# Chunk 1's d_ff tiles 4 to 7 by seven products for eight, chunk 0's block tiles moved ahead of them, and one block's token sums on VectorE

## The chip, the cores and the metric

The kernel runs on one core of one Trainium2 chip. The metric is the device time of one execution in microseconds; the time of the kernel before is the median of three runs. Beside these runs one execution was taken with the hardware profiler, and its trace carries all the rows below.

## The reference

Two stages follow each other. The first is an attention with sketched features, for 4 batches, 4 heads, 1088 tokens and 32 numbers a head; the second is a feed-forward layer with an exact GELU on the 4352 tokens of width 128 that the first one gives.

```python
phi(x) = outer(S1 @ x, S2 @ x)                # 8 x 8 = 64 features a token and head
kv = sum over s of phi(k[s]) v[s];  z = sum over s of phi(k[s])
x  = (phi(q) @ kv) / (phi(q) @ z + 1e-6)      # [4, 4, 1088, 32] -> x [4352, 128]
h  = x @ w_in                                 # [4352, 2048]
out = (0.5 * h * (1 + erf(h / sqrt(2)))) @ w_out   # [4352, 128]
```

`w_in` and `w_out` come as 64-bit floats (the setup multiplies by a 64-bit scalar), so the kernel turns them into 32-bit floats itself, out of their words.

## The kernel before

**Chunks, tiles, steps.** Tokens are worked on in nine chunks: two of 512 tokens for each of the 4 batches (chunks 0 to 7), and one of the 256 tokens left over. For each chunk d_ff is cut into 16 tiles of 128 channels. One *step* t of the main loop is one tile of one chunk: `hidden` (L734; its matmul is L740) multiplies a w_in tile with the chunk's 512 tokens into one of two PSUM banks (`hps`, two buffers), and ScalarE's GELU (L747) takes the bank to SBUF. The list `steps` gives the order of the tiles. Before, it is: chunk 0's tiles 0 to 3 (t = 0 to 3), chunk 1's tiles 0 to 7 (t = 4 to 11), chunk 0's tiles 4 to 15 (t = 12 to 23), chunk 1's tiles 8 to 15 (t = 24 to 31), then the 16 tiles of chunk 2, and so on.

**Two ways for the second product.** The first `USUAL[n]` tiles of chunks 0 and 1 (4 and 8 of them before) go through `project` (L914; matmul L925): one 128x512 product a tile, summed in one bank. All other tiles of chunks 0 to 7 go in *blocks* of four tiles (`NB = 4`) by a scheme with seven products for eight. It needs, for each block, four sums of the tokens' activations (`token_sums`, L783, four GpSimd subtractions or additions of 128x512, L791 to L794) and, for each piece of w_out, four sums of the channels' weights (`channel_sums`, L768, into the tiles `T[1]` to `T[4]`, L778 to L781; the last one, `T[4]`, is needed by the first product of a block). `two_products` (L813, matmul L826) issues two of the 14 products of a block beside each other on the two halves of the array. The two accumulating banks come from the same two-buffer pool (`ops`) as the banks of `project`, so `take_usual` (L852) first copies the usual products away on ScalarE. `drain` (L831) and `combine` (L856) undo the scheme.

**Where the steps' work is put.** Each engine gets its instructions in the order of the text, and keeps that order. `at(t, f, ...)` hangs a call into the list of step t; calls hung into the same step are issued in the order in which the `at` lines stand. In one step the order is: drains, `hidden` with its GELU, `token_sums` of a block whose last tile this was, the step's list, stores, and last the products of `project` and `two_products` that were put into this step.

**The weights.** w_in and w_out lie in five pieces of d_ff (tiles 0-1, 2-3, 4-7, 8-11, 12-15). Pieces 0 and 1 are converted ahead of the loop and in its first steps, pieces 2, 3 and 4 by the list `schedule` (L1146). A piece takes two VectorE instructions on its words (`begin`: L283, L288), two on ScalarE (L270 `low`, L294 `exp`), and three more on VectorE (`end`: L302, L307, L312). The last step of the last piece, the product that makes w_out's tiles 12 to 15, is GpSimd's (`multiply`, L312, hung into step 13). The raw words of pieces 2 to 4 lie in the three buffers of `block`, which the activations of the blocks take over, in that order.

**Around them.** In the same stretch the keys and queries of batch 1 are worked on: `key_turn_blocks` (L383), `features_of_all` (L1043), `outer_of_all` (L1051 to L1058), `turn_keys_rem` and `features_rem` (L348, L421), `add_tokens` (L1067 to L1073), `query_turn` (L554), `z_sum`, `fold_z`, `kv_and_attend` (L456), `query_sketch` (L604), `query_outer` (L616 to L639). `hidden` issues its matmul in two halves of 64 columns from t = 18 on.

The lines that settle GpSimd's order in the stretch of the change:

```python
    at(12, widen_v_rem, 1)
    at(13, multiply, turns[5])
    for i, t in enumerate((5, 6, 14)):
        at(t, channel_sums, i)
    at(16, channel_sums, 3)
```

Of the kernel before, what the change touches and what calls it, by code (L numbers as in the profile page):

```python
# [16 lines left out]
def kernel(  # L17
# [18 lines left out]
    pe, dve, act, pool, sp = nc.tensor, nc.vector, nc.scalar, nc.gpsimd, nc.sync  # L36
# [15 lines left out]
    LAG = 2  # L52
    NMAIN = B * NCH
    NB = 4

    USUAL = [4, 8]
    BLOCKED = 12
    NCHUNK = NMAIN + 1
    assert B == 4 and d_model == 128 == H * D == JC * D == 2 * F and H == 4 and REM == 64 and NCH == 2
# [8 lines left out]
    def work_banks():  # L68

        return wps.tile([128, 2, CW], FP, name="w_ps")  # L70
# [99 lines left out]
    def words(a):  # L170

        return (a, 1) if a.dtype == FP else (a.bitcast(U32), 2)
# [22 lines left out]
    for i, (queue, s) in enumerate(((act, S1), (sp, S2))):  # L195
        s, e = words(s)
# [286 lines left out]
    def turn_kv(b, banks):  # L483

        for rows in (slice(0, 64), slice(64, 128)):
            pe.matmul(banks[rows, 1, :128], lhsT=kv_T[b], rhs=ident, start=True, stop=True)
        act.copy(out=kz[b], in_=banks[:, 1, :128])
# [246 lines left out]
    def hidden(n, fi, by_halves=False):  # L734
# [3 lines left out]
        for rows in (slice(0, 64), slice(64, 128)) if by_halves else (slice(0, 128),):  # L738
            if (n, fi) not in begun:
                pe.matmul(ps[rows, :W], lhsT=w[:, rows], rhs=xT[n][:, :W], start=True, stop=True)  # L740
        if n < NCH and fi < USUAL[n]:
            g_of[n, fi] = mlp.tile([128, CW], FP, name="g", bufs=4)
# [37 lines left out]
        pool.tensor_sub(out=t2, in0=b22, in1=t1)  # L780
        pool.tensor_sub(out=t4, in0=b21, in1=t2)  # L781

    def token_sums(n, b):  # L783

        g = blocks[n, b].rearrange("p (e two) (half x) -> p e two half x", two=2, half=2)
        a11, a21, a12, a22 = (g[:, :, k, h] for k in range(2) for h in range(2))
        s = {}
        for j, (name, dtype) in enumerate((("bits_a", U32), ("bits_e", U32), ("bits_low", FP), ("bits_m", FP))):
            t = mlp.tile([128, LC], dtype, name=name, bufs=3 if dtype == U32 else 2)
            s[j + 1] = (t if dtype == FP else t.bitcast(FP)).rearrange("p (e x) -> p e x", e=2)  # L790
        pool.tensor_sub(out=s[3], in0=a11, in1=a21)  # L791
        pool.tensor_add(out=s[1], in0=a21, in1=a22)  # L792
        pool.tensor_sub(out=s[2], in0=s[1], in1=a11)  # L793
        pool.tensor_sub(out=s[4], in0=a12, in1=s[2])  # L794
        sums[n, b] = s

    def factor(n, b, name, e):
# [12 lines left out]
    def first_block(n):  # L810
        return USUAL[n] // NB if n < NCH else 0

# [39 lines left out]
    def take_usual(n):  # L852
        usual[n] = mlp.tile([128, CW], FP, name="g", bufs=4)
        act.copy(out=usual[n], in_=o_of[n])
# [59 lines left out]
    def project(n, fi, parts=range(B // 2), cols=slice(None)):  # L914
        first, final = fi == (BLOCKED if n == NMAIN else 0), fi == (USUAL[n] if n < NCH else NF) - 1
        if first and n not in o_of:
# [78 lines left out]
    late = []  # L995
# [32 lines left out]

    steps = [(n, fi) for n in range(NCH) for fi in range(USUAL[n])]
    steps += [(n, fi) for n in range(NCHUNK) for fi in range(USUAL[n] if n < NCH else 0, NF)]  # L1030
    slots = {t: [] for t in range(len(steps) + LAG)}

    def at(t, f, *a):
        slots[t].append(lambda: f(*a))
# [40 lines left out]
    held = {}  # L1075
# [67 lines left out]

    turns = [w[i] for i in range(2, 5) for w in (w_in_sb, w_out_sb)]
    both, low, exp = ("low_words", "exponents"), ("low_words",), ("exponents",)
    schedule = ((), ((5, low), (6, exp)), ((7, both),), ((8, low), (9, exp)), ((10, both),), ((11, low), (12, exp)))  # L1146
    for k, acts in enumerate(schedule):
        t1 = acts[-1][0] if acts else 4
        if k + 1 < len(turns):
# [3 lines left out]
        at(t1, end, turns[k], dve if k < 5 else pool)  # L1153
    at(12, widen_v_rem, 1)
    at(13, multiply, turns[5])
    for i, t in enumerate((5, 6, 14)):
        at(t, channel_sums, i)
    at(16, channel_sums, 3)
    for r in range(2):
        at(13, key_turn_blocks, 1, r)  # L1160
    at(15, query_turn, 2)
    at(16, features_of_all, 1)
    at(16, outer_of_all, 1)
    at(16, turn_keys_rem, 1)
    at(17, features_rem, 1)
    at(17, add_tokens, 1)
    at(18, channel_sums, 4)

    at(24, z_sum, 1)
    at(24, fold_z, 1)  # L1170
    at(23, query_turn, 3)
    at(24, kv_and_attend, 1, 1)
    at(24, query_sketch, 2)
    at(26, lambda: turn_kv(1, held["kv"]))
    at(24, query_outer, 2)
    at(6, spread_sketches)
    at(40, repeat_first_z)
    for n in range(3, NCHUNK):

        t = (n - 1) * NF  # L1180
        b = (n + 1) // 2 if n % 2 else n // 2
# [35 lines left out]
                at(t + 10, turn_first_kv)  # L1217


    products = {t: [] for t in range(len(steps) + LAG)}  # L1220
    done = {t: [] for t in range(len(steps) + LAG + 1)}
    drains = {t: [] for t in range(len(steps) + LAG + 1)}
    for t, (n, fi) in enumerate(steps):
        if n < NCH and fi < USUAL[n]:
            products[t + LAG + (0, 0, 0, 0, 0, 1, 2, 2)[fi]].append((project, n, fi))
            if fi == USUAL[n] - 1:
                slots[(13, 17)[n]].append(lambda n=n: take_usual(n))
        elif n == NMAIN:
            if fi % 2 and fi < BLOCKED:
                slots[t].append(lambda k=fi // 2: sums_rem(k))  # L1230
            at_ = t + LAG
            if fi == NF - 1:

                names = [(k, name) for k in range(BLOCKED // 2) for name in ORDER_REM]
                steps_rem = NF - 5
                for i, (k, name) in enumerate(names):
                    products[n * NF + 5 + i * steps_rem // len(names)].append((product_rem, k, name))
                products[n * NF + 4 + steps_rem].append((combine_rem,))

                products[at_] += [(project, n, NF - f, (i,)) for f, i in ((4, 0), (3, 0), (2, 0), (4, 1), (1, 0), (3, 1),  # L1240
                                                                          (2, 1), (1, 1))]
                done[at_ + 1].append(n)
        elif fi % NB == NB - 1:
            b = fi // NB
            opens = b == first_block(n)
            late = int(n < NCH or n == NCH and opens)
            for later, pairs in ((3, 2), (4, 3), (5, 2)) if opens and n == 0 else ((3, 3), (4, 2), (5, 2)) if opens else ((2, 2), (3, 2), (4, 1), (5, 2)):
                later += late
                for i in range(pairs):
                    products[t + later].append((two_products, n, b, len([p for q in products.values() for p in q  # L1250
                                                                        if p[:3] == (two_products, n, b)])))
            if b == NF // NB - 1:
                drains[t + 6 + late].append(n)
                done[t + (12 if n < NMAIN - 1 else 9)].append(n)

    for t in range(len(steps) + LAG):
        if t < 4:

            hidden(0, t)
            if t == 0:  # L1260
                expand_multiply(1, 0)
                w_out[0].fields()
                expand_copy(1, 1)
                expand_multiply(1, 1)
            if t == 1:
                w_out[0].low_words()
                w_out[0].exponents()
                w_out[0].finish()
                w_out[1].fields()
            if t == 2:  # L1270
                w_out[1].low_words()
            if t == 3:
                banks = work_banks()
                numerators_by_token(1, halves(banks), range(JC))
                w_out[1].mantissas(by_pool=True)
                w_out[1].exponents()
                divide(1, halves(banks), 0)
                w_out[1].signs()
                w_out[1].product()
                project(0, 0)  # L1280
                project(0, 1, cols=slice(0, 256))
                turn_half(1, 0, work_bank(), by_act)
                project(0, 1, cols=slice(256, 512))
                turn_half(1, 1, work_bank(), by_dve)
            continue
        if t == 4:
            begin(turns[0])
            by_scalar(turns[0], *both)
            first_hidden(1, 0)
            for f, *a in products[t]:  # L1290
                f(*a)
            first_hidden(1, 1)
        for n in drains[t]:
            drain(n)
        sooner = t == NMAIN * NF
        if sooner:
            for f, *a in products[t]:
                f(*a)
        if t < len(steps):
            n, fi = steps[t]  # L1300
            hidden(n, fi, by_halves=t >= 18)
        if t < len(steps) and steps[t][0] < NMAIN and steps[t][1] % NB == NB - 1:
            n, b = steps[t][0], steps[t][1] // NB
            if b >= first_block(n):
                token_sums(n, b)
        for f in slots[t]:
            f()
        for n in done[t]:
            store(n)
        if t != 4 and not sooner:  # L1310
            for f, *a in products[t]:
                f(*a)
# [41 lines left out]
```

## Time and profile before

| what | value |
|---|---|
| median of 3 runs | 258.2 us (258.13 to 258.35) |
| the profiled execution | 257.65 us, span of its trace 255.9 us |
| TensorE busy in the span | 251.8 us (98%) |
| VectorE, ScalarE, GpSimd busy | 156.9, 114.6, 177.6 us |
| VectorE busy from 20 to 40 us | 18.73 of 20 us |
| GpSimd busy from 40 to 60 us | 18.92 of 20 us |
| granted TensorE clock | 1.00 throughout |

The page names PE for the matmuls of TensorE, PEld for its weight loads, DVE for VectorE, ACT for ScalarE, POOL for GpSimd. A row of the timeline gives the start from the span's beginning, the duration, the engine, the line of the kernel, the operation, the tiles written and read, the shape and the number of instructions merged into the row. The durations of following instructions overlap a little, so what an instruction costs on a busy engine is the distance from its start to the next start.

### The profile page before, as it was taken

What the parts mean: (1) busy time and instruction counts of PE and PEld (TensorE: products, weight loads), DVE (VectorE), ACT (ScalarE), POOL (GpSimd) and SP (SyncE); (2) the same over time, 40 slices, a digit from 0 to 9 for tenths busy, and PEclk for the clock granted to TensorE, in tenths of its full rate; (3) what the DMA queues carried; (4) which work ended last, traced back from release to release, by engine and by line L of the source; (5) the groups of instructions that cost most, each with busy time, mean ns of one, the idle gap of its engine ahead of it and who ended that gap; (6) DMA issues with size and microseconds to landing.
All of it is one profiled execution on the core that took longest, in us unless ns stands there. A gap on an engine that the chain in (4) does not pass through costs nothing.

```text
span 255.9 us, 5994 instructions
## 1 busy us (share of the span) xinstructions
PE 251.8 (98%) x2427; PEld 132.7 (52%) x2427; DVE 156.9 (61%) x331; ACT 114.6 (45%) x221; POOL 177.6 (69%) x194
## 2 busy tenths in 40 slices
PE   8999999999999999999999999999999999999995
PEld 4755444555454546454444455445544444445784
DVE  4899995929798996570278976399507000700382
ACT  3785885323535334533335332623444334433541
POOL 3419329998849776687758874787758777877950
PEclk9999999999999999999999999999999999999999
DMA  6689657810001101111000011000110200020021
GB/s 210 205 267 295 168 116 195 222 31 10 0 3 18 23 4 23 20 19 25 3 0 0 0 17 29 1 4 0 27 16 7 36 1 3 5 36 3 0 35 31
DMA packets 29083, 13.50 MB, mean 53 GB/s; under 512 B 21888, under 2 KB 27264, under 8 KB 29056
## 3 DMA queue, kind: packets, MB, share of 16 engines
q1 hardware_dynamic: 28624, 12.79, 20.5%
q8 instruction: 19, 0.31, 0.5%
q10 hardware_dynamic: 432, 0.33, 0.4%
q14 instruction: 8, 0.07, 0.1%
HBM read 10.88 MB, written 2.23 MB: 51 GB/s over the span
## 4 chain that ended last, share of the span: by engine, by line
PE 98%; ACT 0%; DVE 0%; issue 0%
PE h_ps L740 45%; PE o_ps L826 35%; PE o_ps L925 4%; PE w_ps L896 2%; PE w_ps L456 1%; PE w_ps L604 1%; PE w_ps L659 1%; PE w_ps L957 1%; PE w_ps L570 1%; PE o_ps L922 1%; PE h_ps L756 1%; PE o_ps L445 1%; PE w_ps L1043 1%; PE h_ps L348 1%; PE w_ps L685 0%; PE o_ps L397 0%
## 5 line engine op out<-in xcount | busy, mean ns | idle before, releaser
L740 PE MATMUL h_ps<-xT,w_in 128*64 128x512 f32 (+2 forms) x536 | 138.0, 567 | 0.0
L747 ACT ACTIVATE block<-h_ps 128x512 f32<-128x512 f32 (+1 forms) x132 | 75.4, 572 | 119.5 <-PE h_ps L740 117.6
L826 PE MATMUL o_ps<-block,w_out 128*64 128x256 f32 x232 | 59.5, 379 | 0.0
L791 POOL TENSOR_TENSOR bits_low<-block 128x512 f32<-128x512 f32 x29 | 37.2, 1281 | 28.4 <-ACT block L747 28.4
L740 PEld LDWEIGHTS h_ps<-xT,w_in 128*64 128x64 f32 (+1 forms) x536 | 41.4, 140 | 26.9 <-issue 8.4
L826 PEld LDWEIGHTS o_ps<-block,w_out 128*64 128x64 f32 x232 | 31.7, 137 | 38.6 <-issue 27.4
L792 POOL TENSOR_TENSOR bits_a<-block 128x512 f32<-128x512 f32 x29 | 37.0, 1276 | 12.6 <-ACT block L747 12.6
L841 DVE COPY sums<-o_ps 64x256 f32<-64x256 f32 x8 | 3.3, 417 | 58.9 <-PE o_ps L826 58.9
L793 POOL TENSOR_TENSOR bits_e<-bits_a,block 128x512 f32<-128x512 f32 x29 | 37.3, 1288 | 2.3
L794 POOL TENSOR_TENSOR bits_m<-block,bits_e 128x512 f32<-128x512 f32 x29 | 37.1, 1279 | 2.3
L826 PE MATMUL o_ps<-bits_low,small 128*64 128x256 f32 x116 | 29.9, 380 | 0.0
L826 PE MATMUL o_ps<-block,small 128*64 128x256 f32 x116 | 29.9, 380 | 0.0
L826 PE MATMUL o_ps<-bits_a,small 128*64 128x256 f32 x116 | 29.8, 379 | 0.0
L826 PE MATMUL o_ps<-bits_m,w_out 128*64 128x256 f32 x116 | 29.8, 379 | 0.0
L826 PEld LDWEIGHTS o_ps<-block,small 128*64 128x64 f32 x116 | 15.6, 137 | 18.6 <-issue 11.2
L826 PE MATMUL o_ps<-bits_e,small 128*64 128x256 f32 x116 | 17.7, 383 | 0.0
L826 PEld LDWEIGHTS o_ps<-bits_a,small 128*64 128x64 f32 x116 | 15.8, 137 | 0.5 <-POOL bits_a L792 0.3
L826 PEld LDWEIGHTS o_ps<-bits_m,w_out 128*64 128x64 f32 x116 | 15.9, 137 | 0.0
L826 PEld LDWEIGHTS o_ps<-bits_low,small 128*64 128x64 f32 x116 | 15.6, 137 | 0.4 <-POOL bits_low L791 0.2
L616 DVE STREAM_TRANSPOSE w_ps<-w_ps 128x512 f32<-128x512 f32 (+1 forms) x7 | 4.8, 687 | 17.1 <-ACT xT L670 12.7
L826 PEld LDWEIGHTS o_ps<-bits_e,small 128*64 128x64 f32 x116 | 7.8, 137 | 11.5 <-issue 9.1
L925 PE MATMUL o_ps<-g,w_out 128*128 128x512 f32 (+1 forms) x26 | 12.4, 563 | 0.0
(223 smaller groups left out, 317.8 us busy)
## 6 DMA issues: line engine op xcount, KB each, us to landing
block<-in_moe_w_in_dram SPq DMA_DIRECT2D x3, 512.0 KB, 9.6
block<-in_moe_w_out_dram SPq DMA_DIRECT2D x3, 512.0 KB, 11.6
k<-in_k_dram SPq DMA_DIRECT2D x12, 128.0 KB, 3.2
v<-in_v_dram SPq DMA_DIRECT2D x12, 128.0 KB, 3.2
q<-in_q_dram SPq DMA_DIRECT2D x24, 64.0 KB, 2.5
out_dram<-oT SPq DMA_DIRECT2D x21, 64.0 KB, 2.2
q_first<-in_q_dram SPq DMA_DIRECT2D x2, 256.0 KB, 3.9
v<-in_v_dram SPq DMA_DIRECT2D x2, 256.0 KB, 4.2
```

The source lines that it names most:

```text
L348: pe.transpose(ps[:, i * 128:(i + 1) * 128], in_=s, identity=ident)
L616: dve.transpose(out=tok, in_=ps[:, :, :H2])
L740: pe.matmul(ps[rows, :W], lhsT=w[:, rows], rhs=xT[n][:, :W], start=True, stop=True)
L747: act.activation(out=g_of[n, fi][:, :W], in_=ps[:, :W], func=ACT.Gelu)
L791: pool.tensor_sub(out=s[3], in0=a11, in1=a21)
L792: pool.tensor_add(out=s[1], in0=a21, in1=a22)
L793: pool.tensor_sub(out=s[2], in0=s[1], in1=a11)
L794: pool.tensor_sub(out=s[4], in0=a12, in1=s[2])
L826: pe.matmul(acc[n][bank][half * 64:(half + 1) * 64, col:col + HW], lhsT=fixed, rhs=moving, start=opens and e == 0 and name in "4715", stop ...
L841: dve.tensor_copy(out=N[lo, 0, one], in_=a0[lo, one])
L896: pe.matmul(acc[NMAIN][rows, COLS_REM[name]], lhsT=tokens[:, rows], rhs=fixed, start=k == 0 and name == ORDER_REM[0], stop=k == BLOCKED // ...
L925: pe.matmul(o_of[n][:, cols], lhsT=w_tile(w_out_sb, fi), rhs=g[:, cols], start=first, stop=final)
```

## The change

`USUAL` becomes `[4, 4]`: chunk 1's tiles 4 to 7 become a block. The order of the steps follows from it: chunk 0's tiles 0 to 3 (t = 0 to 3), chunk 1's tiles 0 to 3 (t = 4 to 7), chunk 0's tiles 4 to 15 (t = 8 to 19), chunk 1's tiles 4 to 15 (t = 20 to 31). The four usual products of chunk 1 go into steps 6, 8, 12 and 15. A table `BEHIND` gives the steps of the block products of chunk 0's three blocks and of chunk 1's first two; the first pair of products is in step 17 (step 19 before). The sums of chunk 0's first block are issued on VectorE, in step 14, after `key_turn_blocks`. The conversion of the last two pieces, the channel sums and the work on batch 1's keys and queries move by a step or a few. Chunk 0's drain goes from step 30 to step 28 and its store from step 35 to step 31.

```diff
-    USUAL = [4, 8]
+    USUAL = [4, 4]
...
-    def token_sums(n, b):
+    def token_sums(n, b, eng=pool):
...
-        pool.tensor_sub(out=s[3], in0=a11, in1=a21)
-        pool.tensor_add(out=s[1], in0=a21, in1=a22)
-        pool.tensor_sub(out=s[2], in0=s[1], in1=a11)
-        pool.tensor_sub(out=s[4], in0=a12, in1=s[2])
+        eng.tensor_sub(out=s[3], in0=a11, in1=a21)
+        eng.tensor_add(out=s[1], in0=a21, in1=a22)
+        eng.tensor_sub(out=s[2], in0=s[1], in1=a11)
+        eng.tensor_sub(out=s[4], in0=a12, in1=s[2])
...
-    schedule = ((), ((5, low), (6, exp)), ((7, both),), ((8, low), (9, exp)), ((10, both),), ((11, low), (12, exp)))
+    schedule = ((), ((5, low), (6, exp)), ((7, both),), ((8, low), (9, exp)), ((11, low), (12, exp)),
+                ((12, low), (13, exp)))
...
     at(12, widen_v_rem, 1)
     at(13, multiply, turns[5])
-    for i, t in enumerate((5, 6, 14)):
+    for i, t in enumerate((5, 6, 13, 14, 18)):
         at(t, channel_sums, i)
-    at(16, channel_sums, 3)
     for r in range(2):
         at(13, key_turn_blocks, 1, r)
-    at(15, query_turn, 2)
-    at(16, features_of_all, 1)
-    at(16, outer_of_all, 1)
-    at(16, turn_keys_rem, 1)
-    at(17, features_rem, 1)
-    at(17, add_tokens, 1)
-    at(18, channel_sums, 4)
-
-    at(24, z_sum, 1)
-    at(24, fold_z, 1)
-    at(23, query_turn, 3)
-    at(24, kv_and_attend, 1, 1)
-    at(24, query_sketch, 2)
-    at(26, lambda: turn_kv(1, held["kv"]))
-    at(24, query_outer, 2)
+    at(14, token_sums, 0, 1, dve)
+    at(17, features_of_all, 1)
+    at(17, outer_of_all, 1)
+    at(17, turn_keys_rem, 1)
+    at(18, features_rem, 1)
+    at(18, add_tokens, 1)
+    at(18, query_turn, 2)
+
+    at(22, query_turn, 3)
+    at(23, z_sum, 1)
+    at(23, fold_z, 1)
+    at(23, kv_and_attend, 1, 1)
+    at(23, query_sketch, 2)
+    at(25, lambda: turn_kv(1, held["kv"]))
+    at(23, query_outer, 2)
...
+    BEHIND = {(0, 1): (17, (2, 3, 2)), (0, 2): (20, (2, 2, 1, 2)), (0, 3): (24, (2, 2, 1, 2)), (1, 1): (30, (4, 3)),
+              (1, 2): (32, (3, 4))}
...
-            products[t + LAG + (0, 0, 0, 0, 0, 1, 2, 2)[fi]].append((project, n, fi))
+            products[t + LAG + n * (0, 1, 4, 6)[fi]].append((project, n, fi))
             if fi == USUAL[n] - 1:
-                slots[(13, 17)[n]].append(lambda n=n: take_usual(n))
+                slots[(14, 16)[n]].append(lambda n=n: take_usual(n))
...
+            if (n, b) in BEHIND:
+                spread_over = [(BEHIND[n, b][0] + i, pairs) for i, pairs in enumerate(BEHIND[n, b][1])]
...
-                drains[t + 6 + late].append(n)
+                drains[t + 6 + late if n else 28].append(n)
...
-            if b >= first_block(n):
+            if b >= first_block(n) and (n, b) != (0, 1):
                 token_sums(n, b)
```

## The prediction

> **What bounds the kernel now.** I read the page's busy times first, then the chain that ended last, then the timelines of PE, DVE, ACT and POOL from 16 to 70 us, the stretch that the change reorders.
>
> ```profile
> span 255.9 us, 5994 instructions
> ...
> PE 251.8 (98%) x2427; PEld 132.7 (52%) x2427; DVE 156.9 (61%) x331; ACT 114.6 (45%) x221; POOL 177.6 (69%) x194
> ...
> PE 98%; ACT 0%; DVE 0%; issue 0%
> ```
>
> PE is the bound: the chain is 98% PE. Between 20 and 240 us I found no distance between two matmul starts longer than the columns need, apart from some 0.05 to 0.15 us at each change of the array's tile shape. So each matmul saved there is saved in the time, and each wait added is added.
>
> ```profile
> 34.88 1.02 PE L925 MATMUL o_ps<-g,w_out 128*128 128x512 f32 x2
> 35.73 1.88 PE L740 MATMUL h_ps<-xT,w_in 128*128 128x512 f32 x4
> 37.45 1.02 PE L925 MATMUL o_ps<-g,w_out 128*128 128x512 f32 x2
> ...
> 42.86 1.94 PE L740 MATMUL h_ps<-xT,w_in 128*64 128x512 f32 x8
> 44.62 0.38 PE L826 MATMUL o_ps<-block,small 128*64 128x256 f32 x1
> ```
>
> Start to start, a usual product costs 0.86 us, a hidden tile 0.86 (34.88 to 35.73; 35.73 to 37.45 for two), a pair of block products 0.43 (two of them lie between 44.62 and 45.49). The last row is the first block product of the kernel, in step 19.
>
> **What the change removes from PE.** Four usual products, 4 x 0.86 = 3.44 us, give way to one block of seven pairs, 7 x 0.43 = 3.01. That is -0.43 us, all of it on the bound, and the most that the change can bring. One piece goes the other way: `features_rem` (L421) now runs in step 18, between matmuls of 64 columns, so two changes of shape come in where there was one: about +0.13 us by the excess at such changes (0.09 to 0.15).
>
> **When PE comes to the first block product.** It is in step 17 now. Before it PE had 16 hidden tiles (steps 4 to 19), ten usual products and L421; now 14 tiles and six products. It comes 6 x 0.86 + 0.3 = 5.5 us earlier, at 39.2 us. On the way ScalarE costs a little: in steps 8 to 11 there is one usual product instead of four, so tiles come 0.86 us apart, while ScalarE issues a GELU (0.49 start to start), a `low` (0.57) or an `exp` (0.66) in turn, and a third tile must wait until a bank is free. Going through its queue I get the tile of step 12 about 0.5 us late, and the first block product at 39.8. This hangs on what follows and is not added to it.
>
> **When that product can start.** Its first operand is `T[4]`, the last of the four channel sums of piece 2. GpSimd issues those behind `multiply`, both in step 13 and in this order, as before (there in 13 and 14); and `multiply` waits for VectorE's last step on piece 4 (L307).
>
> ```profile
> 36.01 0.78 DVE L302 SCALAR_TENSOR_TENSOR bits_m<-bits_a,bits_low 128x512 f32<-128x512 uint32 x1
> 36.71 0.68 DVE L307 SCALAR_TENSOR_TENSOR bits_e<-block,bits_r 128x512 uint32<-128x512 uint32 x1
> 37.31 1.29 DVE L383 STREAM_TRANSPOSE kT<-k 128x512 f32<-128x512 f32 x2
> 38.54 0.66 DVE L554 STREAM_TRANSPOSE qT<-q 128x512 f32<-128x512 f32 x1
> ```
>
> ```profile
> 37.47 1.33 POOL L312 TENSOR_TENSOR w_out<-bits_m,bits_e 128x512 f32<-128x512 f32 x1 [1.23 <-DVE bits_e L307]
> 38.74 0.47 POOL L778 TENSOR_TENSOR small<-w_out 128x128 f32<-128x128 f32 x1
> ...
> 40.11 0.45 POOL L781 TENSOR_TENSOR small<-w_out,small 128x128 f32<-128x128 f32 x1
> 40.52 1.28 POOL L791 TENSOR_TENSOR bits_low<-block 128x512 f32<-128x512 f32 x1
> ```
>
> VectorE is the engine behind this: from 21.6 to 39.2 us it has no idle row, and the change keeps the order of its conversions, so L307 of the last piece cannot end before 37.4. ScalarE's `low` and `exp` still reach it in time by the same walk (the last `exp` ends at about 35.9, L307 starts at 36.71). So `T[4]` is ready at 40.56 at the earliest (40.11 + 0.45). Before, PE came for it at 44.62, four microseconds later. Now PE stands before it from 39.2 or 39.8 on, and with it everything queued behind: the rest of the block products and the hidden tiles, and so ScalarE's GELUs.
>
> **What the sums on VectorE add.** They stand behind `key_turn_blocks`, where `query_turn` stood (38.54), just when GpSimd comes to the channel sums. Each has two inputs in SBUF, as have GpSimd's. The trace of before has VectorE and GpSimd at such work at the same time in `combine`:
>
> ```profile
> 74.92 1.39 DVE L860 TENSOR_TENSOR sums<-sums 64x256 f32<-64x256 f32 x1
> 76.33 0.42 DVE L861 TENSOR_TENSOR sums<-sums 64x256 f32<-64x256 f32 x1
> 76.78 1.65 DVE L863 TENSOR_TENSOR sums<-sums,g 128x512 f32<-128x512 f32 x1
> ```
>
> ```profile
> 76.48 1.39 POOL L792 TENSOR_TENSOR bits_a<-block 128x512 f32<-128x512 f32 x1 [0.45 <-ACT block L747]
> 77.96 1.62 POOL L793 TENSOR_TENSOR bits_e<-bits_a,block 128x512 f32<-128x512 f32 x1
> ```
>
> The 0.42 us instruction takes 1.39 when it meets one of GpSimd's, and ends 0.28 us after that one (76.03); L863 takes 1.65 instead of 0.69 and ends 0.56 us after GpSimd's (77.87); then GpSimd's next takes 1.62 instead of 1.28 and ends 1.15 us after VectorE's. They take turns, one whole instruction each; two later passes of `combine` (93 and 148 us) show the same. The Trainium skill's page "SBUF — State Buffer", section "Who interferes with whom", calls it an exclusive lock on a shared port pair that an instruction with two SBUF inputs holds to its end; by it the move to VectorE does not come free, the trace agrees with 1.39 against 0.42, and the sum would be 261.1 us by the lock and 259.4 without.
>
> So: `multiply` ends at 38.80. Then in turn a VectorE sum (0.56) and a channel sum (0.46 less the 0.13 by which a held GpSimd instruction is shorter, 0.33), four times: 4 x 0.89 = 3.5 us, and `T[4]` is ready at 42.3. Without any contention it is 40.56; if VectorE got all its four sums in first (0.56 + 3 x 0.61, then 4 x 0.44), 43.0. I take 42.3, because each pair in the rows alternates. With some 0.15 us to the weight load and the matmul the first block product starts at 42.45 (bounds 40.7 and 43.1).
>
> **The sum.** Before, that product started at 44.62; now 2.17 us earlier. But from there to the end PE has more to do than it had: two hidden tiles (1.72), one block more (3.01), and L421 with its changes of shape (0.4): 5.13 us. The net is 5.13 - 2.17 = +2.96 us. The other way round: -0.43 + 0.13 + (42.45 - 39.2). The profiled execution is 257.65 us, a span of 255.9 and 1.75 around it; its forecast is 260.6. The median of the runs lies 0.55 above it, so the number for the median is 258.2 + 2.9 = 261.1.
>
> **What else moves, at nothing.** The later block products: behind `T[4]` GpSimd makes piece 3's sums (to 44.1) and (0, 2)'s token sums (first one 45.4, last 49.3); PE comes to them in step 20 at 48.5 and step 23 at about 55. Chunk 0's third block (sums to 56.2, needed from 57) and (1, 1) (to 61.4, needed at 65.3) follow. `add_tokens` ends on VectorE near 51, `z_sum` stands in step 23 near 53. Chunk 0's drain in step 28 needs 3.1 us on VectorE in before (65.17 to 68.24); two tiles and the first three pairs, which go to the bank that is free sooner, cover it, with about 0.3 us to spare, and that is the price if VectorE is late. Tiles 8 and 12 of w_in end on VectorE at 30.8 and 36.0 and are now needed at 31.4 and 36.6 or later; the buffers of raw words are free at 27.5, 32.8 and 37.4, against GELUs that come at 29.1, 33 and 38.1. Margins of half a microsecond: if one fails it mostly eats into the wait that comes anyway. The sixteen DMAs of chunk 0's store are only issued earlier, on a queue that is empty by then (its last loads are issued by 60 us).
>
> **Rivals.** (1) The wait without the contention: the first product starts at 40.7, the net is 5.13 - 3.92 = +1.2, so 259.4 us. Against it stand the alternating rows; for it, that channel sums are only 128 wide and might slip between. (2) Not slower: `T[4]` is there before PE. Then only -0.43 + 0.13 is left, 257.9 us. This decides at 39.2 us: GpSimd would have to begin `multiply` by 36 us, or the channel sums would have to stand ahead of it. The order of the calls and VectorE's full queue speak against it. (3) More is lost: VectorE gets all its sums in first, or a late conversion shifts the chain by another 0.5 us: 261.7 us.
>
> **The numbers.** Chances: forecast 0.58, (1) 0.18, (2) 0.12, (3) 0.12. Likeliest 261.1. The range takes in (1) with 0.2 us below it and (3) with 0.4 above: 259.2 to 262.1, leaving out (2) and the unforeseen. A measurement of this kernel can tell about 0.2%, 0.5 us, from no change. Case (2) is within that in most of its outcomes: faster 0.05, same 0.08, slower 0.87.
>
> **What would show it.** In the timeline of PE after: an idle stretch of 2.5 to 3 us ahead of the first row of L826, in step 17, ended by POOL's L781; that row at 42.4 us. On DVE four rows of 0.9 us spacing from 38.5 us, between them on POOL L778 to L781 at the same spacing (0.42 now). The hidden tiles of steps 9 to 12 a few tenths apart from 0.86. Then PE without gaps to 240 us. I am wrong if the first L826 follows the matmul ahead of it directly, if L781 ends before 40.5 us, or if PE waits again behind step 17.

## The result and the profile after

The changed kernel takes 262.37 us (median of 5 runs, 260.38 to 262.69) against 258.35 us before: a ratio of 1.015, 95% interval 1.0115 to 1.0185. It is slower, as forecast, but by 4.0 us instead of 2.9, and it lies 0.3 us above the range. The five runs are of two kinds, and the number can't be read without that: one of 260.38 us, with the granted clock at 1.0, and four of 262.3 to 262.7, with a mean granted clock of 0.993 (a sixth execution on record, outside the median, took 262.61 at 0.993). The profile is of the first kind, a span of 258.6 us.

From the page of that profile, the busy times and the engines' shares of the chain that ended last:

```profile
span 258.6 us, 6042 instructions
...
PE 252.3 (98%) x2447; PEld 132.5 (51%) x2447; DVE 157.9 (61%) x335; ACT 114.0 (44%) x221; POOL 179.6 (69%) x194
...
PE 86%; DMA 5%; SPq 5%; POOL 2%; issue 0%; DVE 0%; ACT 0%; POOLq 0%
```

The chain was 98% PE; it now leaves PE through POOL and goes back into the loads of the inputs (DMA and SPq, SyncE's queue). Where it leaves, PE's timeline shows (steps 16 and 17, then the first block product):

```profile
37.29 1.88 PE L740 MATMUL h_ps<-xT,w_in 128*128 128x512 f32 x4
39.10 0.67 PE L1043 MATMUL w_ps<-kT,S_ab 64*32 64x256 f32 x16
39.70 0.33 PE L348 MATMUL w_ps<-ident,k_rem 128*128 128x128 f32 x1
42.34 0.43 PE L826 MATMUL o_ps<-block,small 128*64 128x256 f32 x1 [2.32 <-POOL small L781]
```

2.32 us of idle time ahead of the first block product, ended by the last channel sum. GpSimd's and VectorE's timelines give the reason:

```profile
37.54 1.30 POOL L312 TENSOR_TENSOR w_out<-bits_m,bits_e 128x512 f32<-128x512 f32 x1
38.80 0.90 POOL L778 TENSOR_TENSOR small<-w_out 128x128 f32<-128x128 f32 x1
39.67 0.90 POOL L779 TENSOR_TENSOR small<-w_out 128x128 f32<-128x128 f32 x1
40.53 0.90 POOL L780 TENSOR_TENSOR small<-w_out,small 128x128 f32<-128x128 f32 x1
41.51 0.78 POOL L781 TENSOR_TENSOR small<-w_out,small 128x128 f32<-128x128 f32 x1
42.25 0.45 POOL L778 TENSOR_TENSOR small<-w_out 128x128 f32<-128x128 f32 x1
```

```profile
36.74 0.69 DVE L307 SCALAR_TENSOR_TENSOR bits_e<-block,bits_r 128x512 uint32<-128x512 uint32 x1
37.34 1.30 DVE L383 STREAM_TRANSPOSE kT<-k 128x512 f32<-128x512 f32 x2
38.56 0.83 DVE L791 TENSOR_TENSOR bits_low<-block 128x512 f32<-128x512 f32 x1
39.31 0.94 DVE L792 TENSOR_TENSOR bits_a<-block 128x512 f32<-128x512 f32 x1
40.29 0.82 DVE L793 TENSOR_TENSOR bits_e<-bits_a,block 128x512 f32<-128x512 f32 x1
41.15 0.83 DVE L794 TENSOR_TENSOR bits_m<-block,bits_e 128x512 f32<-128x512 f32 x1
```

Piece 2's channel sums take 0.78 to 0.90 us each where they took 0.46; piece 3's, from 42.25 on, when VectorE is done with its sums, 0.45 again. L307 ends at 37.43, as before (37.39); `T[4]` is there at 42.29 instead of 40.56.

### The profile page after: what moved, and what is told of

Read it like the earlier page. It is cut to its first block, busy times and chain, and to the rows that moved or that the text cites. A ratio compares the mean times of both kernels' runs of the same rounds, so it can differ in the third digit from the quotient of the medians.

```text
span 258.6 us, 6042 instructions
## 1 busy us (share of the span) xinstructions
PE 252.3 (98%) x2447; PEld 132.5 (51%) x2447; DVE 157.9 (61%) x335; ACT 114.0 (44%) x221; POOL 179.6 (69%) x194
## 4 chain that ended last, share of the span: by engine, by line
PE 86%; DMA 5%; SPq 5%; POOL 2%; issue 0%; DVE 0%; ACT 0%; POOLq 0%
PE h_ps L740 39%; PE o_ps L826 36%; DMA k<-in_k_dram 4%; PE w_ps L896 2%; PE w_ps L456 1%; PE w_ps L604 1%; PE w_ps L659 1%; PE w_ps L957 1%; SPq L189 1%; SPq L125 1%; SPq L109 1%; DMA v_rem<-in_v_dram 1%; SPq L136 1%; PE o_ps L922 1%; SPq L181 1%
## 5 line engine op out<-in xcount | busy, mean ns | idle before, releaser
L747 ACT ACTIVATE block<-h_ps 128x512 f32<-128x512 f32 (+1 forms) x136 | 77.9, 573 | 123.8 <-PE h_ps L740 121.6
L826 PE MATMUL o_ps<-block,w_out 128*64 128x256 f32 x240 | 61.9, 379 | 0.0
L791 POOL TENSOR_TENSOR bits_low<-block 128x512 f32<-128x512 f32 x29 | 37.6, 1296 | 29.4 <-ACT block L747 29.4
L740 PEld LDWEIGHTS h_ps<-xT,w_in 128*64 128x64 f32 (+1 forms) x536 | 40.6, 140 | 28.6 <-issue 7.1
L826 PEld LDWEIGHTS o_ps<-block,w_out 128*64 128x64 f32 x240 | 32.6, 137 | 38.9 <-issue 27.4
L793 POOL TENSOR_TENSOR bits_e<-bits_a,block 128x512 f32<-128x512 f32 x29 | 37.0, 1276 | 2.3
L826 PE MATMUL o_ps<-block,small 128*64 128x256 f32 x120 | 30.9, 380 | 2.3 <-POOL small L781 2.3
L826 PE MATMUL o_ps<-bits_a,small 128*64 128x256 f32 x120 | 31.2, 379 | 0.0
L826 PE MATMUL o_ps<-bits_low,small 128*64 128x256 f32 x120 | 30.9, 380 | 0.0
L826 PE MATMUL o_ps<-bits_m,w_out 128*64 128x256 f32 x120 | 30.8, 379 | 0.0
L826 PEld LDWEIGHTS o_ps<-block,small 128*64 128x64 f32 x120 | 16.2, 137 | 22.1 <-issue 12.1
L826 PE MATMUL o_ps<-bits_e,small 128*64 128x256 f32 x120 | 18.3, 383 | 0.0
L826 PEld LDWEIGHTS o_ps<-bits_m,w_out 128*64 128x64 f32 x120 | 16.4, 137 | 0.0
L826 PEld LDWEIGHTS o_ps<-bits_a,small 128*64 128x64 f32 x120 | 16.2, 137 | 0.0
L826 PEld LDWEIGHTS o_ps<-bits_low,small 128*64 128x64 f32 x120 | 16.2, 137 | 0.0
L826 PEld LDWEIGHTS o_ps<-bits_e,small 128*64 128x64 f32 x120 | 8.1, 137 | 11.3 <-issue 9.1
L1067 DVE TENSOR_REDUCE w_ps<-k_p 128x128 f32<-128x1024 f32 x6 | 11.9, 1982 | 0.2
```

Of the source, the lines that this page charges most:

```text
L747: act.activation(out=g_of[n, fi][:, :W], in_=ps[:, :W], func=ACT.Gelu)
L791: eng.tensor_sub(out=s[3], in0=a11, in1=a21)
L793: eng.tensor_sub(out=s[2], in0=s[1], in1=a11)
L826: pe.matmul(acc[n][bank][half * 64:(half + 1) * 64, col:col + HW], lhsT=fixed, rhs=moving, start=opens and e == 0 and name in "4715", stop ...
L1067: dve.tensor_reduce(out=sums[:, c], in_=k_p[b][c].rearrange("p n r f -> p (r f) n"), axis=mybir.AxisListType.X, op=AX.add)
```

## The experiments

All are made from the changed kernel. Ratios are to the kernel before; that kernel, run beside them on the same chips, has medians of 258.09 us (up to the products put later) and 258.13 (the last two runs). Executions differ by up to 0.9 us in when the first hidden tile starts (13.86 to 14.74 us in these traces), so part of a difference between two traces can lie ahead of it.

**The changed kernel once more**, to have the long execution in a trace.

> The changed kernel itself, once more, for a profile of an execution at the longer time. Theory G (the clock gate): most executions take 262.3 to 262.7 us with a mean granted clock of 0.993, some 260.4 with 1.0; where the clock is below 1.0 the trace shows PE rows of about twice their duration for 3 to 4 us, beginning within a few us behind the wait for T[4] in step 17, and nowhere else. Rival theory R (something other than the clock makes the 2 us, a DMA that lands late for example): matmul rows keep their durations and a second wait of about 2 us shows.

262.19 us (261.88 to 262.48, 4 runs), all with the clock at 0.993. The wait is the same, 2.25 us up to 42.86. Then the engines by stretches of time (after the length come the busy times of PE, PEld, DVE, ACT and POOL, each with its count; the third number from the end is the granted clock):

```profile
42.00:43.00 1.00, 0.14 (x2) 0.14 (x4) 1.00 (x2) 0.00 (x0) 0.98 (x2) 1.00 0.54 157
43.00:44.00 1.00, 1.00 (x10) 0.71 (x10) 0.93 (x3) 0.00 (x0) 1.00 (x3) 0.88 0.52 137
44.00:47.00 3.00, 3.00 (x10) 1.06 (x10) 2.40 (x4) 0.79 (x2) 2.92 (x4) 0.50 0.73 216
47.00:48.00 1.00, 1.00 (x10) 0.57 (x8) 1.00 (x1) 0.00 (x0) 0.92 (x2) 0.92 0.96 225
```

and the same execution's PE rows:

```profile
43.77 1.93 PE L740 MATMUL h_ps<-xT,w_in 128*64 128x512 f32 x4
45.63 0.69 PE L421 MATMUL w_ps<-S,kT_rem 128*128 128x64 f32 x2
46.25 1.08 PE L826 MATMUL o_ps<-bits_e,small 128*64 128x256 f32 x4
...
48.03 1.02 PE L740 MATMUL h_ps<-xT,w_in 128*64 128x512 f32 x4
```

About 0.9 us behind the wait the clock is at one half for 3.4 us (0.24 in the second row, 3.0, 0.16), and a hidden tile takes 1.93 us instead of 1.03. Half of 3.4 is the loss, 1.7 us. The span of this trace, 260.7 us, is 2.1 us longer than that of the first profile; the other 0.5 lies ahead of the wait's end, at 42.86 here and at 42.34 there. Theory R (a second wait) falls: PE has no other idle stretch in the loop.

**Five matmuls on zeros into the wait.**

```diff
+        if t == 17:
+            keep_busy(5, hidden_bank())
         if t != 4 and not sooner:
             for f, *a in products[t]:
```

> Five matmuls on noughts (128x256, 0.43 us each, 2.15 us together) are put ahead of the first block product in step 17, into a hidden bank that is free; nothing else changes. Theory G: PE waits for T[4] all the same and the first block product stays at 42.3 to 42.5 us, but the array isn't idle and the clock stays at 1.0: 260.4 to 260.6 us in all executions, 2 us below the changed kernel's median. Theory R: the 2 us stay, 262.4 us.

260.57 us (260.28 to 260.98, 5 runs), the clock at 0.999 to 1.0 in all; ratio to before 1.0097 (1.0084 to 1.0110). PE in step 17:

```profile
39.76 0.33 PE L348 MATMUL w_ps<-ident,k_rem 128*128 128x128 f32 x1
39.93 2.34 PE L957 MATMUL h_ps<-const-float32-0.0 128*128 128x256 f32 x10
42.46 0.43 PE L826 MATMUL o_ps<-block,small 128*64 128x256 f32 x1 [0.19 <-POOL small L781]
```

The first block product waits for the same L781, to 42.46. Only the idle time is gone, and with it 1.6 us of the median: work that does nothing makes the kernel faster. So the 4.1 us of the changed kernel beside these runs are two losses: 2.5 us of waiting, net of what the block saves, and 1.6 us of lowered clock that the waiting sets off (1.7 by the trace).

**Two fillers, one filler** (`keep_busy(2, ...)`, `keep_busy(1, ...)`), to see how much waiting lowers the clock.

> As the kernel with five fillers, with two (0.86 us) ahead of the first block product: PE is idle for 1.4 us instead of 2.3. The trace with the low clock had 2.25 idle us in one 3.41 us window of the clock's record, the profiled execution at full clock 1.55 in one and 0.77 in the next. Theory G with a bound between these two: no fall, 260.3 to 260.7 us in all executions. Rival: any wait in step 17 over about a microsecond lowers the clock in most executions, median 262.0 or more.

> One filler (0.43 us): PE is idle for 1.85 us. By theory G the bound lies between 1.55 and 2.25 idle us in one window: if it is below 1.85, some executions fall to 262 us and some stay at 260.4, by where the wait lies in the window; if above, all stay at 260.4. Without theory G the executions stay with those of the changed kernel, 262.2.

With two, 1.51 us idle in the trace: 260.95 us (260.35 to 261.16, 4 runs), the clock never under 0.998. With one, 1.87 us idle: 261.11 us, six executions, of which two have 0.993 (262.41 and 262.58) and four 1.0 (260.25 to 261.19). With none, 2.3 us, nine of the ten executions of the changed kernel on record fell. In these runs a longer wait brought more falls.

What decides in one execution is not shown, but the traces narrow it down. The clock's record falls once more behind the end of each span, where TensorE is idle: in the trace with the low clock at 262.21 us, 218.45 us or 64 times 3.413 us behind the fall at 43.76. The rise at 47.17 is one such step behind it, so its changes lie on a grid of 3.413 us there. Counted back from that last fall in each trace, the wait that lowered the clock lay whole in one interval of the grid (40.34 to 43.76, 2.25 idle us in it). In the changed kernel's profiled execution, which kept its clock, the last fall is at 260.02 us and the grid cuts the wait at 41.57 into 1.55 and 0.77 us; in the profiled execution with one filler, which kept it too, the last fall is at 259.80 and the cut at 41.35, into 0.98 and 0.89. That fits a bound on the idle time in one interval, between 1.55 and 2.25 us. It rests on one trace with a fall; no run was made to place the wait in the grid.

**Three of the four VectorE sums later**, behind the channel sums.

```diff
         eng.tensor_sub(out=s[3], in0=a11, in1=a21)
-        eng.tensor_add(out=s[1], in0=a21, in1=a22)
...
+        if eng is dve:
+            held["rest"] = rest        # s[1], s[2], s[4]; called in outer_of_all behind L1054
```

> Of the four sums on VectorE only the first stays in step 14; the other three follow L1054 of outer_of_all, behind the channel sums in time. Theory of the alternating port: only one VectorE sum gets between the channel sums, T[4] is ready at 41.2 to 41.5 us (42.29 in the changed kernel) and the fast execution takes 259.4 to 259.7 us. Rival (the channel sums are slow for another reason): L778 to L781 stay at 0.9 us each and the first product at 42.3. With a wait of 1.4 us instead of 2.3 theory G leaves open whether the clock still falls; without a fall all executions agree within 0.3 us.

259.29 us (258.99 to 259.89, 6 runs), ratio 1.0052 (1.0039 to 1.0066), no fall of the clock; a little less than expected. GpSimd's timeline:

```profile
38.69 0.90 POOL L778 TENSOR_TENSOR small<-w_out 128x128 f32<-128x128 f32 x1
39.55 0.45 POOL L779 TENSOR_TENSOR small<-w_out 128x128 f32<-128x128 f32 x1
39.97 0.45 POOL L780 TENSOR_TENSOR small<-w_out,small 128x128 f32<-128x128 f32 x1
40.49 0.45 POOL L781 TENSOR_TENSOR small<-w_out,small 128x128 f32<-128x128 f32 x1
40.91 0.93 POOL L778 TENSOR_TENSOR small<-w_out 128x128 f32<-128x128 f32 x1
```

Only the channel sum that meets the one remaining VectorE sum takes 0.9 us. `T[4]` is ready at 40.94 (expected 41.2 to 41.5), the wait is 1.12 us. The slow rows have moved to piece 3's sums (from 40.91), where nobody waits. So in this stretch a channel sum is slow where a VectorE sum meets it, and only there.

**Piece 2's channel sums ahead of `multiply`.**

```diff
-    for i, t in enumerate((5, 6, 13, 14, 18)):
+    for i, t in enumerate((5, 6, 8, 14, 18)):
```

> The channel sums of piece 2 go from step 13 to step 8, so GpSimd issues them ahead of multiply, where it was idle. Theory of the wait: T[4] is ready by 32 us and the first block product waits only for VectorE's first sum, which the four channel sums delay by up to 1 us: it starts at 39.8 to 40.6 us instead of 42.34, and the time is 258.0 to 258.8 us with the clock at 1.0 in all executions. Rival (the wait is not GpSimd's channel sums but what lies around them): 260.4 us or more.

259.67 us (259.27 to 259.98, 5 runs), 0.9 us above the upper end of what was expected. The wait for `T[4]` is gone (the first block product follows L348 at 41.35; in this execution the first hidden tile already comes 0.64 us later than in that of the changed kernel, so it is 1.6 us sooner). But two new waits come in, in PE's timeline:

```profile
36.86 1.12 PE L740 MATMUL h_ps<-xT,w_in 128*128 128x512 f32 x2 [0.47 <-ACT block L747]
...
54.12 0.67 PE L604 MATMUL w_ps<-qT,S_abc 64*32 64x256 f32 x16 [0.46 <-DVE S_abc L514]
```

The sums, put where GpSimd was idle, meet VectorE's conversions (L302 and L307 take 0.94 us there instead of 0.69) and delay them by 0.9 us; a GELU then waits 0.73 us for L307 to free a buffer of raw words, and PE for its bank. And with the first block earlier, `query_sketch` in step 23 comes to `fold_z` too soon.

**The sums back on GpSimd.**

```diff
-    at(14, token_sums, 0, 1, dve)
+    at(13, token_sums, 0, 1)
```

> The move to VectorE is undone: (0, 1)'s sums are GpSimd's, behind piece 2's channel sums (0.45 us each again, T[4] at 40.6) and ahead of piece 3's. The first product (T[4]) starts at 40.8, its partner waits for the first token sum to 41.9, the later ones stand 0.5 us behind in step 18, and everything on GpSimd comes 3.4 us later than in the changed kernel, with waits of 0.5 to 2 us more in steps 20 to 30. In sum 260.5 to 262.5 us, with or without a fall of the clock. If VectorE's sums were the whole loss it would be below 259.4 us.

261.6 us (261.18 to 261.68, 4 runs), ratio 1.0132 (1.0117 to 1.0147), the clock at 0.998 to 1.0. The channel sums take 0.46 us again, and PE's one wait becomes three, of 0.73, 0.58 and 0.28 us (L781, L791, L793). That is 1.0 us more than with the fillers, where the clock doesn't fall either. Between the two profiled executions 0.7 us of it lies ahead of the first hidden tile, where the kernels are the same. Behind it the three waits cost no more than the one: it is the second block, whose first token sum GpSimd now ends at 49.60 us, that loses another 0.4 us: one product starts at 49.22, its partner on the other half of the array at 49.66. So the move to VectorE isn't the mistake, and the block is too early for either engine.

**Products and sums later.** Made from the kernel with three sums later.

```diff
-    BEHIND = {(0, 1): (17, (2, 3, 2)), ...
+    BEHIND = {(0, 1): (18, (2, 5)), ...
```

> The kernel with three sums later, and besides (0, 1)'s products go from steps 17 to 19 (2, 3, 2 pairs) to steps 18 and 19 (2 and 5). PE comes to the first block product at 41.0 to 41.2 us, T[4] is ready at 40.94, so the wait of 1.12 us is gone. Theory: what is left against the kernel before is -0.43 for the block, +0.13 for the shapes and about +0.5 for ScalarE's queue in steps 9 to 13: 257.9 to 258.5 us, no measurable difference to before. Rival (the 0.43 us comes through in full once T[4] is there): 257.6 or less.

258.91 us (258.45 to 259.16, 6 runs), ratio 1.0031 (1.0020 to 1.0042), 0.4 us above the expectation. The wait for `T[4]` is gone, and again L604 waits, 0.43 us for L514. So the next kernel puts `z_sum` and what hangs on it back into step 24:

```diff
-    at(23, z_sum, 1)      # and fold_z, kv_and_attend, query_sketch, query_outer
-    at(25, lambda: turn_kv(1, held["kv"]))
+    at(24, z_sum, 1)
+    at(26, lambda: turn_kv(1, held["kv"]))
```

> The kernel with three sums and the first block's products later had one more wait in its trace: 0.44 us ahead of L604 (query_sketch) in step 23, for VectorE's fold_z. Here z_sum, fold_z, kv_and_attend, query_sketch and query_outer of batch 1 go back from step 23 to 24 and turn_kv from 25 to 26, as in the kernel before. Theory (waits on the bound add up one by one): that wait goes, 258.2 to 258.6 us, against 258.9 measured without it. Rival (it only moves on): 258.9 again.

258.29 us (257.80 to 258.93, 12 runs), ratio 1.0009 (0.9997 to 1.0021), within what was expected: the whole change without its waits on `T[4]` and `fold_z`, and no measurable difference to before. One more attempt is made from this kernel:

```diff
-    at(17, turn_keys_rem, 1)
-    at(18, features_rem, 1)
+    at(16, turn_keys_rem, 1)
+    at(17, features_rem, 1)      # ahead of features_of_all
...
-                slots[(14, 16)[n]].append(lambda n=n: take_usual(n))
+                slots[(17, 16)[n]].append(lambda n=n: take_usual(n))
```

> Besides, features_rem (L421) goes from step 18 to 17 and turn_keys_rem (L348) from 17 to 16, so the array changes its shape less often between matmuls of 64 columns, and chunk 0's usual products are copied away in step 17 instead of 14, out of ScalarE's full stretch. Theory: 0.1 to 0.4 us less than the kernel it is made from, 257.9 to 258.4 us: at best within 0.2% of the kernel before, since ScalarE's queue in steps 9 to 13 still takes what the block gives (0.43). Rival (the block's 0.43 us comes through): below 257.6 us.

258.69 us (258.31 to 259.10, 12 runs), ratio 1.0023 (1.0013 to 1.0033), 0.4 us slower than the one it is made from, against an expected gain of 0.1 to 0.4. PE's timeline has a wait for the moved VectorE sums (the lines are numbered anew in this kernel: L833 is the changed kernel's L826, L796 its L793):

```profile
44.11 0.65 PE L833 MATMUL o_ps<-bits_e,small 128*64 128x256 f32 x4 [0.30 <-DVE bits_e L796]
```

`features_rem` now puts its VectorE step (L427) ahead of them, and L427 waits 0.83 us for ScalarE's copy. No kernel here beats the one before.

## Why the prediction was right and wrong

**The wait, right.** `T[4]` at 42.3 (measured 42.29), the first block product at 42.45 (42.34), the tile of step 12 late by 0.5 us through ScalarE (the four tiles of steps 9 to 12 take 3.91 us instead of 3.44), PE at the first block product at 39.8 (L348, the matmul ahead of it, ends at 40.03). The profiled execution, forecast at 260.6, is 260.38. Rival (1), no contention, is refuted by the 0.90 us rows and by the kernel with three later sums; rival (2) by the idle 2.32 us; of rival (3), the sums come in turn and L307 is not late. Nothing else waits behind step 17, as forecast.

**The sum, wrong by one term.** "From there to the end PE has more to do than it had ... 5.13 us" was priced by rows at full clock, and the clock behind the wait was put at nothing. In the trace with the low clock 3.4 us of that work run at half clock, which costs 1.7 us (1.6 by the fillers), and 261.1 becomes 262.8; measured 262.37. Four of the five runs have the mean clock of 0.993 that goes with it. At full clock the sum was 0.2 to 0.5 us too high: 260.6 against 260.38 in the profiled execution, 261.1 against the 260.57 with five fillers; so part of the miss is hidden by an error the other way. The trace of before had no idle stretch of PE of that length inside the loop, so it could not show the fall. But the forecast itself made one of more than 2 us, and there it should have given the work behind the wait two prices, at full and at lowered clock; rival (3) named only more waiting.

**The rule of a page.** The Trainium skill's page "TensorE: Matmul & The Clock Gate", section "Part 1: The HAM clock gate (the "warmup" mystery)", says that the clock is halved after an idle window of about 3.4 us of a free-running counter, and given back after a busy one. The length agrees with the 3.4 us at 0.50. That a wait must fill a window does not: 2.3 us were enough in nine executions of ten, and 1.9 us in two of six.

**The gain, never seen alone.** With all waits on `T[4]` and `fold_z` taken away the change ends at 1.0009 of before. Whether the block's -0.43 us is in it was not measured. ScalarE's queue is: the four tiles of steps 9 to 12 take 3.91 us in that trace too (29.36 to 33.27) instead of 3.44, and the extra change of shape was left in as well. That these two offset the gain, and are the whole of it, is argued from rows and not shown by a run.

## What to carry to other kernels

On a kernel whose TensorE never waits, find for each product that is moved ahead the queue that makes its last operand, and read when that row ends now: an engine that is 69% busy over the span can be the one that is late in the stretch that matters. Two engines whose instructions take turns are not two engines; beside a sum that TensorE waits for, put none on the other engine. And a wait of TensorE of some 2 us can have a second price, the clock behind it; where the wait can't be avoided, a few matmuls on zeros paid for themselves here.

## What the runs showed of the hardware

A wait of 2.3 us lowered the clock in nine of ten executions; in the one trace that shows it, the granted clock is 0.50 for 3.4 us, beginning about 0.9 us after TensorE is back at work. Waits of 1.51 and 1.12 us did not lower it in ten executions. Between VectorE and GpSimd, each at instructions with two inputs in SBUF, whole instructions alternate: a channel sum of 0.46 us takes up to 0.90, and a VectorE sum 0.82 to 0.94 where one that meets none takes 0.68 (the second of the four, in the kernel with three sums later).
